# Depthwise weight gradient of a convolutional gate: products and sums on GpSimd in place of 128x128 products on TensorE, with new leads for the planner

## The chip, the cores and the metric

The kernel runs on one core of a Trainium2 chip. The metric is the device time of one execution in microseconds, as the median of several runs; a profile of one further execution shows where its time goes. PE is TensorE, PEld its weight loads, DVE VectorE, ACT ScalarE, POOL GpSimd, SP SyncE.

## The reference, cut to what matters

The reference is the forward pass and all gradients of an E-Branchformer block for B = 2 sequences of T = 4000 rows and D = 144 channels, in bf16. A global branch is attention; a local branch is a gated MLP whose gate is a depthwise convolution with K = 5 taps along the rows:

```python
xc = _layernorm(x, axis=-1)
h = _gelu(jnp.einsum('btd,de->bte', xc, w_mlp_in))
u, g = (h[..., :D].copy(), h[..., D:].copy())
g = _layernorm(g, axis=-1)
gp = jnp.pad(g, ((0, 0), (pad, pad), (0, 0)))
gc = jnp.zeros_like(g)
for i in range(K):
    gc = gc + gp[:, i:i + T, :] * dw_csgu[i][None, None, :]
loc = jnp.einsum('btd,de->bte', u * gc, w_mlp_out)
...
_out, _vjp = jax.vjp(_f, x, w_qkv, w_att_out, w_mlp_in, dw_csgu, w_mlp_out, dw_merge, w_merge)
_grads = _vjp(grad_out)
```

The change concerns the gradient of `dw_csgu`, a 5x144 result: for tap i and channel c it is the sum over all 8000 rows of gp[row + i, c] times dgc[row, c], where dgc is the gradient that reaches gc.

## The kernel before, in words

Rows are laid out in 32 blocks of 125 partitions per sequence (PB = 125, NB = 32), partition p of block j holding row 32 p + j, so that a shift by one row is a shift by one block, and halos are needed only at the ends. The kernel has a head (weights, layer norm, transposes), then one long loop over the 64 query blocks of both sequences (`phase_att`), and an end in which the merge convolution, the output, dx and the remaining weight gradients are computed.

In step s of the loop, TensorE makes the scores of block s and the dP tiles of block s-1 (`quad`: four products of 500 columns on L1254, then four of 16 rows on L1261, into the PSUM tiles `ps`, of which there are two). VectorE takes each score tile out with its negated minimum (`S_min`, L1276, into Pbuf); ScalarE takes the exponential (L1282); the dP tile is multiplied by P, either by VectorE straight from PSUM (L1290) or by ScalarE's copy (L1292) and a VectorE product in SBUF (L1294). Pbuf and Sbuf go through DMA transposes into PT and ST, from which `Y_half` (L1303) and `Z_half` (L1341) sum over 32 blocks. `X_group` (L1385) sums the gradient of the normalised input, which VectorE adds to `acc` (L1391). GpSimd makes small operands on the way: qr (L1237), QBs (L1321 to L1325).

Beside it, in the steps that are set aside for it, run the "local units" (`local_units`), 16 rounds of two blocks per batch, one batch after the other. In a round, blocks of a new pair n get their gelu and its derivative (L576 to L637, with the tiles l_hs, l_sq, l_a, l_z, l_th, l_q, l_hg), the normalised gate and dgc, which go side by side into a ring of tiles `gd` (gd[:, 0] the gate, gd[:, 1] dgc; five slots and three fixed ones for the ends), and the last 16 channels also into `gd_rem`. `t_unit` transposes them, `gc_unit` and `dgn_unit` make the convolution and its adjoint for an older pair o, `dhT_unit` transposes the gradient of h (dhr), and `dwi_unit` makes the gradient of w_mlp_in.

The weight gradient of the gate is made in `dwc_unit`, in every second round, over four blocks. For each block and tap it makes the 128x128 product of the shifted gate with dgc on TensorE; of this product only the diagonal is wanted. Part 0 holds four taps in one PSUM tile `pw` of 128x512 (L728), part 1 the fifth tap (L730) and one 80x144 product for the last 16 channels of all five taps (L731). `flush` copies the tile to `l_fl` with ScalarE (L710) and adds it to the accumulator `A_dwc` (128x784, f32) with GpSimd (L711). At the end `Final.dwc` takes the diagonals out: VectorE multiplies by the identity (L1873) or a mask (L1874) with a running sum, casts to bf16, two transposes on TensorE turn the columns into rows, and six transfers write the 5x144 result. `dwi_unit` uses `flush` as well, with 96x432 tiles.

The order of the work on each engine isn't the order of the program. `Planner.plan` takes the instructions from step 2 on, groups PE's, gives each group a duration from a table of costs (`cost`, and the lines at L1025 for groups), and lays them out one after another by a list schedule: of the groups that are ready it takes the one with the least key, and the key is its place in the program plus a lead from the table LEAD, by engine, output tile and size ("A" keys before the end stage, "T" keys in it). The chosen order is then fixed on every engine.

Of the kernel before, what the change touches and what calls it, by code (L numbers as in the profile page):

```python
# [8 lines left out]
BF = mybir.dt.bfloat16  # L9
F32 = mybir.dt.float32  # L10
ACT = mybir.ActivationFunctionType
ALU = mybir.AluOpType
# [3 lines left out]
D = 144  # L16
DR = 16
PB = 125
# [510 lines left out]
G2 = 2  # L529
# [4 lines left out]
def local_units(k, W, b, S, A, es, DHT, ps_w, gw):  # L534

    nc, tc = k.nc, k.tc
# [3 lines left out]
    pl = es.enter_context(tc.tile_pool(name="loc%d" % b, bufs=1, side=side, reuse_waits="tile"))  # L540
# [3 lines left out]
    rem = pl.tile([PB, 2, NB + 4, DR], BF, name="gd_rem")  # L544

    def gd(c):
        return gdr[{0: NR, NG2: NR + 1, NG2 + 1: NR + 2}.get(c, c % NR)]
    for c in (0, NG2 + 1):
        lo = 0 if c == 0 else 96
        nc.gpsimd.memset(gd(c)[lo:(32 if c == 0 else PB)], 0.0)  # L550
    gT = [pl.tile([128, 4, PB], BF, name="gT%d" % i) for i in range(4)]
# [11 lines left out]
    gc = pl.tile([PB, G2, D], BF, name="l_gc")  # L563
    dd = pl.tile([PB, G2, 2 * D], BF, name="l_dd")
    w_ = pl.tile([PB, G2, D], F32, name="l_w")
    fl = pl.tile([128, 512], F32, name="l_fl")

    def slot(g):
        return 3 if g == NG2 - 1 else g % 3
# [138 lines left out]
    def flush(ps, rows, acc):  # L708
        n = ps.shape[1]
        nc.scalar.copy(fl[0:rows, 0:n], ps)  # L710
        nc.gpsimd.tensor_tensor(acc, fl[0:rows, 0:n], acc, op=ALU.add)  # L711

    def blocks(g):
        return [(g - 1, 0), (g - 1, 1), (g, 0), (g, 1)]

    def gnb(h):
        return gd(h // G2)[:, 0, h % G2, 0:128]

    def dwc_unit(g, part):
        pw = ps_w.tile([128, 512], F32, tag="w")  # L720
        bl = blocks(g)
        for n_, (gg, bi) in enumerate(bl):
            i = G2 * gg + bi
            first, last = n_ == 0, n_ == len(bl) - 1
            t = gd(gg + 1)
            if part == 0:
                for kk in range(4):
                    nc.tensor.matmul(pw[:, kk * 128:(kk + 1) * 128], gnb(i + kk), t[:, 1, bi, 0:128], start=(first and kk == 0), stop=last, skip_group_check=True)  # L728
            else:
                nc.tensor.matmul(pw[:, 0:128], gnb(i + 4), t[:, 1, bi, 0:128], start=first, stop=last, skip_group_check=True)  # L730
                nc.tensor.matmul(pw[0:80, 128:128 + D], rem[:, 0, i:i + 5, :].rearrange("p a b -> p (a b)"), t[:, 1, bi, :], start=False, stop=last, skip_group_check=True)  # L731
        if part == 0:
            flush(pw[:], 128, A.dwc[:, 0:512])
        else:
            flush(pw[:, 0:128], 128, A.dwc[:, 512:640])
            flush(pw[0:80, 128:128 + D], 80, A.dwc[0:80, 640:784])

    def dwi_unit(g):
        pw = ps_w.tile([96, 3 * D], F32, tag="w")
# [12 lines left out]
    def round_(n, o, c):  # L752

        new = [(z_unit, n, 0), (z_unit, n, 1), (e_tanh, n), (e_h, n), (e_stats, n), (dug_unit, n), (e_gn, n), (e_dgc, n), (e_m, n), (e_gp, n)]
        old = [(gc_unit, o), (e_du, o), (dgn_unit, o), (e_dh, o)]
        end = [(dhT_unit, o)]
        if o is not None and o % 2:
            end += [(dwc_unit, o, 0), (dwc_unit, o, 1), (dwi_unit, o)]
        tr = [(t_unit, c, c - 2 if c is not None and c >= 2 else None)]
        if n is None:  # L760
            new = [None] * 10
        if o is None:
            old, end = [None] * 4, [None]
        if c is None:
            tr = [None]
        for u_ in (new[0:3] + old[0:1] + new[3:5] + old[1:2] + new[5:7] + old[2:3] + new[7:9] + old[3:4] + new[9:10] + tr + end):
            if u_ is not None:
                add(*u_)
# [11 lines left out]
class Planner:  # L780


    LEAD = {
# [13 lines left out]
    }  # L797


# [114 lines left out]
    def plan(self, i0, i1, window=400, late=1 << 40):  # L914
# [38 lines left out]
        for ins in todo:  # L953
            if ins.name not in gof:
                continue
            g = gof[ins.name]
# [66 lines left out]
        for g in groups:  # L1023
            d, end = 0.0, 0.0
            if g["e"] == "PE" and g["sg"]:  # L1025
                m = [i for i in g["ins"] if i.ins[0].bass_ap.ap[0][1] >= 128]
                if len(m) < len(g["ins"]):
                    d = len(m) * 0.21 + 0.094 + 0.22 + 0.14
                    end = d - 0.14 + 0.22
                else:  # L1030
                    d = len(m) * 0.21
                    end = d + 0.17
            else:
                for i in g["ins"]:
                    b, l = self.cost(g["e"], i)
                    end = d + l
                    d += b
            g["d"], g["end"] = d, end
        succ = [[] for _ in groups]
        need = [len(p) for p in preds]  # L1040
# [755 lines left out]
class Final:  # L1796
# [68 lines left out]
    def dwc(self):  # L1865

        k, nc, A, fp, W = self.k, self.k.nc, self.A, self.fp, self.W
        dwc_c = fp.tile([128, 5], F32, name="dwc_c")
        dwc_s = fp.tile([80, 1], F32, name="dwc_s")
        self.jf = jf = fp.tile([128, D], F32, name="jf")  # L1870
        av = A.dwc
        for kk in range(5):
            nc.vector.scalar_tensor_tensor(jf[:, 0:128], av[:, kk * 128:(kk + 1) * 128], 1.0, W.ident[:], op0=ALU.mult, op1=ALU.mult, accum_out=dwc_c[:, kk:kk + 1])  # L1873
        nc.vector.scalar_tensor_tensor(jf[0:80, 0:DR], av[0:80, 640 + 128:640 + D], 1.0, W.mask[:], op0=ALU.mult, op1=ALU.mult, accum_out=dwc_s[:])  # L1874
        dwc_b = fp.tile([128, 5], BF, name="dwc_b")
        nc.vector.tensor_copy(dwc_b[:], dwc_c[:])
        dwc_sb = fp.tile([80, 1], BF, name="dwc_sb")
        nc.vector.tensor_copy(dwc_sb[:], dwc_s[:])
        pt = self.pt([5, 128], BF)
        nc.tensor.transpose(pt[:], dwc_b[:], W.ident[:])  # L1880
        o5 = fp.tile([5, 128], BF, name="o5")
        nc.scalar.copy(o5[:], pt[:])
        nc.sync.dma_start(k.out5[:, 0:128], o5[:])
        pt = self.pt([1, 80], BF)
        nc.tensor.transpose(pt[:], dwc_sb[:], W.ident[0:80, 0:80])
        o5s = fp.tile([1, 5, DR], BF, name="o5s")
        nc.scalar.copy(o5s[:].rearrange("p a b -> p (a b)"), pt[:])
        for kk in range(5):
            nc.sync.dma_start(k.out5[kk:kk + 1, 128:D], o5s[:, kk, :])

    def qk(self):
        k, nc, A, fp, W = self.k, self.k.nc, self.A, self.fp, self.W
# [88 lines left out]
def kernel(ctx, tc, x, w_qkv, w_att_out, w_mlp_in, dw_csgu, w_mlp_out, dw_merge, w_merge, grad_out,  # L1981
# [47 lines left out]
    A = K()  # L2029
    A.dM1T = ap.tile([128, 2, D], F32, name="A_dM1T")  # L2030
    A.dWiT = ap.tile([96, 3 * D], F32, name="A_dWiT")
    A.dwc = ap.tile([128, 784], F32, name="A_dwc")
    k.ps_w = pool(ctx, "ps_w", "left", bufs=3, space=PSUM)
    k.ps_yz = pool(ctx, "ps_yz", "left", bufs=1, space=PSUM)
    W = K()
# [114 lines left out]
    F = Final(k, W, A, ar, fp)  # L2150
    F.ps = K()
    F.ps.tile = lambda shape, dt, tag=None, name=None, bufs=None: k.ps_w.tile(shape, dt, tag="w", name=name)
    side += [F.dwc, F.dwi, F.weights]
    for q, f in enumerate(M.tr_pieces(1)):
        f()
# [66 lines left out]
```

## Time and profile before

| | us |
|---|---|
| median of three runs | 1304.31 |
| lowest and highest | 1299.45, 1305.04 |
| the profiled execution | 1301.2 |
| its span in the profile | 1299.4 |
| PE idle in the span | 40.3 |
| products into pw from gd (L728, L730, L731), instructions | 384 |
| copies to l_fl for them (L710) | 18.2 |
| sums into A_dwc (L711) | 38.3 |

An instruction's row gives the smallest, the median and the largest duration, or the mean; a product on PE has a span of about 0.22 us, but products overlap, and the distance from one start to the next is what each takes of PE's time. Busy time on PE counts the union of such spans. A line "A <- B: us, times, longest" says how long engine A stood idle before an instruction and whose result ended that idle time.

### The profile page before, as it was taken

The page shows a single profiled execution, that of the slowest core. Times are in us where ns is not written, and L with a number is a line of the kernel's source. Part 1 is how long each engine was busy: PE and PEld are TensorE (multiplying, and loading weights), DVE is VectorE, ACT ScalarE, POOL GpSimd, SP SyncE. Part 2 cuts the span into 40 slices and gives each one's busy share as a digit, 9 for nine tenths or more (in the row PEclk, how much of TensorE's full clock was granted, in tenths as well). Part 3 has the DMA queues.
Part 4 walks back from the last instruction along what each step waited for, and adds up shares of the span by engine and source line. Part 5 has one row for each costly group of instructions (what it writes and reads, how often), then busy time and mean ns, then how long its engine had stood idle before and what let it go on. Part 6 is the DMA issues. An engine that isn't in the chain of part 4 may idle for free.

```text
span 1299.4 us, 39889 instructions
## 1 busy us (share of the span) xinstructions
PE 1259.1 (97%) x16190; PEld 1045.8 (80%) x16190; DVE 1053.7 (81%) x2808; ACT 828.5 (64%) x1384; POOL 505.6 (39%) x1013
## 2 busy tenths in 40 slices
PE   5999999999999999999999999999999999999998
PEld 3677888888888887877778888888888878799997
DVE  7589888888889888888978898888888887767925
ACT  4776676676676776556756767667566666436561
POOL 8654434443444433331444434344443423143310
PEclk8999999999999999999999999999999999999999
DMA  4587787687677687979987688777676868958702
GB/s 121 103 143 128 129 142 134 117 151 125 126 135 132 121 140 148 162 137 162 180 145 130 124 144 122 130 127 139 123 136 123 137 120 153 185 121 219 204 25 58
DMA packets 585444, 175.45 MB, mean 135 GB/s; under 512 B 560813, under 2 KB 579663, under 8 KB 585239
## 3 DMA queue, kind: packets, MB, share of 16 engines
q1 hardware_dynamic: 583544, 171.31, 71.6%
q8 instruction: 126, 2.06, 0.6%
q0 software_dynamic: 1168, 1.39, 0.4%
q14 instruction: 58, 0.48, 0.1%
q10 hardware_dynamic: 548, 0.21, 0.1%
HBM read 22.96 MB, written 16.69 MB: 31 GB/s over the span
## 4 chain that ended last, share of the span: by engine, by line
PE 87%; DVE 4%; DMA 2%; ACT 2%; POOL 2%; issue 2%; SPq 1%; ACTq 0%; DVEq 0%; POOLq 0%
PE X L1385 21%; PE ps L1254 15%; PE yz L1341 10%; PE yz L1303 9%; PE ps L1261 6%; PE Hps L1673 3%; PE po L1758 2%; PE pd L611 1%; PE pc L663 1%; PE pj L1227 1%; PE pd L678 1%; PE pt L1243 1%; ACT Pbuf L1282 1%; PE pw L728 1%; DVE Pbuf L1276 1%
## 5 line engine op out<-in xcount | busy, mean ns | idle before, releaser
L1276 DVE TENSOR_SCALAR_CACHE_REDUCE Pbuf<-ps 125x1000 bf16<-125x1000 f32 x256 | 306.4, 1197 | 92.3 <-PE ps L1261 87.5
L1282 ACT ACTIVATE Pbuf<-Pbuf,nm 125x1000 bf16<-125x1000 bf16 x256 | 282.6, 1134 | 79.0 <-DVE nm L1278 79.0
L1385 PE MATMUL X<-QBs,Sbuf 125*125 125x144 bf16 x2048 | 296.3, 228 | 0.3 <-ACT l_sq L579 0.2
L1385 PE MATMUL X<-QBs,Pbuf 125*125 125x144 bf16 x2048 | 291.4, 226 | 1.5 <-POOL QBs L1325 1.5
L1385 PEld LDWEIGHTS <-Sbuf 125*125 125x125 bf16 x2048 | 259.4, 137 | 20.8 <-issue 20.8
L1254 PE MATMUL ps<-xaT_m,qt 128*125 128x500 bf16 x1024 | 261.8, 375 | 2.5 <-ACT Sbuf L1292 1.2
L1385 PEld LDWEIGHTS <-Pbuf 125*125 125x125 bf16 x2048 | 260.5, 137 | 0.6 <-issue 0.5
L1292 ACT CAST Sbuf<-ps 125x1000 bf16<-125x1000 f32 x190 | 189.6, 998 | 100.1 <-PE ps L1261 99.8
L1391 DVE TENSOR_TENSOR acc<-X,acc 125x432 f32<-125x432 f32 (+1 forms) x373 | 201.4, 550 | 31.5 <-PE X L1385 27.8
L1254 PEld LDWEIGHTS <-qt 128*125 128x125 bf16 x1024 | 121.5, 136 | 43.3 <-issue 4.7
L1341 PE MATMUL yz<-xa_aug,ST 125*125 125x144 bf16 x2048 | 150.9, 228 | 3.9 <-ACT ty L1319 3.0
L1303 PE MATMUL yz<-xa_aug,PT 125*125 125x145 bf16 x2048 | 147.7, 227 | 4.2 <-DMA PT<-Pbuf 4.2
L1341 PEld LDWEIGHTS <-ST 125*125 125x125 bf16 x2048 | 139.9, 138 | 6.5 <-issue 5.5
L1303 PEld LDWEIGHTS <-PT 125*125 125x125 bf16 x2048 | 137.3, 137 | 8.3 <-DMA PT<-Pbuf 5.4
L1294 DVE TENSOR_TENSOR Sbuf<-Sbuf,Pbuf 125x1024 bf16<-125x1024 bf16 x190 | 134.6, 711 | 9.5 <-ACT Sbuf L1292 9.4
L1261 PEld LDWEIGHTS <-qt 16*125 16x125 bf16 x1024 | 36.6, 128 | 99.1 <-issue 98.4
L1261 PE MATMUL ps<-XR,qt 16*125 16x500 bf16 x1016 | 112.1, 420 | 0.0
L1321 POOL TENSOR_SCALAR QBs<-qb,rl 125x144 bf16<-125x144 bf16 x64 | 26.1, 408 | 181.4 <-DVE rl L1309 160.7
L1290 DVE TENSOR_TENSOR Sbuf<-ps,Pbuf 125x1000 bf16<-125x1000 f32 x66 | 78.8, 1194 | 6.5 <-PE ps L1261 3.4
L711 POOL TENSOR_TENSOR A_dwc<-l_fl,A_dwc 128x512 f32<-128x512 f32 (+2 forms) x48 | 38.3, 798 | 90.2 <-ACT l_fl L710 89.8
L1237 POOL COPY qr<-qb 125x64 bf16<-125x64 bf16 x124 | 31.9, 284 | 77.8 <-ACT qb L1229 75.3
L581 POOL TENSOR_SCALAR l_a<-l_sq 125x576 bf16<-125x576 bf16 x32 | 21.5, 672 | 95.4 <-ACT l_sq L579 94.7
(579 smaller groups left out, 2508.8 us busy)
## 6 DMA issues: line engine op xcount, KB each, us to landing
Yn_d<-yn SPq DMA_DIRECT2D x64, 35.2 KB
Zn_d<-zn SPq DMA_DIRECT2D x64, 35.2 KB
ug_d<-ugr SPq DMA_DIRECT2D x32, 70.3 KB
PT<-Pbuf SPq DMA_TRANSPOSE x126
ST<-Sbuf SPq DMA_TRANSPOSE x126
go_h<-in_grad_out_dram SPq DMA_DIRECT2D x8, 252.0 KB
Yg<-Yn_d SPq DMA_DIRECT2D x8, 252.0 KB
Yg<-ug_d SPq DMA_DIRECT2D x8, 252.0 KB
```

The costliest lines, as they stand in the source:

```text
L1254: mm = nc.tensor.matmul(pp[r // 2][:, r % 2, 0:CH], QT[i][:, 3 * h, :], bs(i)[0].xaT_m[:, c * CH:(c + 1) * CH], start=True, stop=False)
L1261: nc.tensor.matmul(pp[r // 2][:, r % 2, 0:CH], QT[i][rs, 1 + (q // 2 + h) % 2, :], xr, start=False, stop=True)
L1276: nc.vector.tensor_scalar(pv(Pbuf, i % NPB, c2), src, -1.0, 3.0e38, op0=ALU.mult, op1=ALU.min, accum_out=NM[i][:, c2:c2 + 1])
L1282: nc.scalar.activation(v, v, ACT.Exp, bias=NM[i][:, 4:5], scale=-1.0)
L1290: nc.vector.tensor_tensor(pv(Sbuf, i % NDB, c2), src, pv(Pbuf, i % NPB, c2), op=ALU.mult)
L1292: nc.scalar.copy(pv(Sbuf, i % NDB, c2), src)
L1294: nc.vector.tensor_tensor(sc, sc, pchunk(i % NPB, c2), op=ALU.mult)
L1303: nc.tensor.matmul(Y, PT[0:PB, j, 0:PB], S.xa_aug[:, j, 0:D + 1], start=(j == 0), stop=(j == NB - 1))
L1341: nc.tensor.matmul(Z, ST[0:PB, j, 0:PB], S.xa_aug[:, j, 0:D], start=(j == 0), stop=(j == NB - 1))
L1385: nc.tensor.matmul(X[:, jj, :], l, r, start=(n_ == 0), stop=(n_ == len(ops) - 1))
L1391: nc.vector.tensor_tensor(av, X[:, 0:nj, :], av, op=ALU.add)
L1673: nc.tensor.matmul(H[0:rows, a // 3, (a % 3) * D:(a % 3 + 1) * D], lhs, self.src[b][h][:, 2 + j, :], start=(n == 0 and a % 3 == 0), stop=( ...
```

## The change

`dwc_unit` no longer uses TensorE. It is called for each single block (twice in every round, where before two parts were called in every second round). GpSimd multiplies the gate, shifted by each of the five taps, with dgc, element by element over all 144 channels, into a new tile `l_pr` (125x5x144, f32): the taps of one gate tile go together, so that a block takes three products, two over 2x144 columns and one over 144. A fourth instruction adds l_pr to `A_dwc`, which now is 125x5x144 in f32. The sum over the 125 partitions is left to the end: `Final.dwc` splits A_dwc into a high and a low bf16 part on VectorE, in pieces of three and two taps, and TensorE multiplies both with a column of ones (the column D of xa_aug, `F.one`), giving one row of 432 or 288; ScalarE copies it out, and two transfers write the result.

`l_fl` shrinks to what `dwi_unit` needs. The table LEAD is replaced as a whole; in the planner's costs a group of quads with remainders gets 0.02 us more, and each PE group 0.02 us more.

```diff
-    fl = pl.tile([128, 512], F32, name="l_fl")
+    fl = pl.tile([96, 3 * D], F32, name="l_fl")
+    pr = pl.tile([PB, 5, D], F32, name="l_pr")
...
-    def dwc_unit(g, part):
-        pw = ps_w.tile([128, 512], F32, tag="w")
-        bl = blocks(g)
-        for n_, (gg, bi) in enumerate(bl):
-            i = G2 * gg + bi
-            first, last = n_ == 0, n_ == len(bl) - 1
-            t = gd(gg + 1)
-            if part == 0:
-                for kk in range(4):
-                    nc.tensor.matmul(pw[:, kk * 128:(kk + 1) * 128], gnb(i + kk), t[:, 1, bi, 0:128], start=(first and kk == 0), stop=last, skip_group_check=True)
-            else:
-                nc.tensor.matmul(pw[:, 0:128], gnb(i + 4), t[:, 1, bi, 0:128], start=first, stop=last, skip_group_check=True)
-                nc.tensor.matmul(pw[0:80, 128:128 + D], rem[:, 0, i:i + 5, :].rearrange("p a b -> p (a b)"), t[:, 1, bi, :], start=False, stop=last, skip_group_check=True)
-        if part == 0:
-            flush(pw[:], 128, A.dwc[:, 0:512])
-        else:
-            flush(pw[:, 0:128], 128, A.dwc[:, 512:640])
-            flush(pw[0:80, 128:128 + D], 80, A.dwc[0:80, 640:784])
+    def dwc_unit(g, bi):
+        i, t = G2 * g + bi, gd(g + 1)
+        kk = 0
+        while kk < 5:
+            h = i + kk
+            n = min(2 - h % 2, 5 - kk)
+            nc.gpsimd.tensor_tensor(pr[:, kk:kk + n, :], gd(h // G2)[:, 0, h % G2:h % G2 + n, :], t[:, 1, bi:bi + 1, :].to_broadcast([PB, n, D]), op=ALU.mult)
+            kk += n
+        nc.gpsimd.tensor_tensor(A.dwc[:], pr[:], A.dwc[:], op=ALU.add)
...
-        if o is not None and o % 2:
-            end += [(dwc_unit, o, 0), (dwc_unit, o, 1), (dwi_unit, o)]
+        if o is not None:
+            end += [(dwc_unit, o, 0), (dwc_unit, o, 1)]
+            if o % 2:
+                end += [(dwi_unit, o)]
...
     LEAD = {
-        "A PE ps 0 0": -120, "A DVE Pbuf 1000 0": 25, "A DVE Sbuf 1024 0": 175, "A PE ph 0": 40, "A ACT l_hs 288": 106, "A ACT l_sq 288": -167,
...
+        "A PE ps 0 0": -77, "A DVE Pbuf 1000 0": 135, "A ACT Sbuf 1000 0": 42, "A DVE Sbuf 1024 0": 178, "A PE ph 0": -199, "A ACT l_hs 288": -38,
...
-                    d = len(m) * 0.21 + 0.094 + 0.22 + 0.14
+                    d = len(m) * 0.21 + 0.094 + 0.22 + 0.16
                     end = d - 0.14 + 0.22
...
+                if g["e"] == "PE":
+                    d, end = d + 0.02, end + 0.02
...
-        for kk in range(5):
-            nc.vector.scalar_tensor_tensor(jf[:, 0:128], av[:, kk * 128:(kk + 1) * 128], 1.0, W.ident[:], op0=ALU.mult, op1=ALU.mult, accum_out=dwc_c[:, kk:kk + 1])
-        nc.vector.scalar_tensor_tensor(jf[0:80, 0:DR], av[0:80, 640 + 128:640 + D], 1.0, W.mask[:], op0=ALU.mult, op1=ALU.mult, accum_out=dwc_s[:])
...
-        for kk in range(5):
-            nc.sync.dma_start(k.out5[kk:kk + 1, 128:D], o5s[:, kk, :])
+        self.jf = fp.tile([128, D], F32, name="jf")
+        for a0, a1 in ((0, 3), (3, 5)):
+            n = (a1 - a0) * D
+            av = A.dwc[:, a0:a1, :].rearrange("p a b -> p (a b)")
+            hi, lo = (fp.tile([PB, 3 * D], BF, tag="dwc_%s" % t, name="dwc_%s" % t) for t in ("hi", "lo"))
+            nc.vector.tensor_copy(hi[:, 0:n], av)
+            nc.vector.tensor_tensor(lo[:, 0:n], av, hi[:, 0:n], op=ALU.subtract)
+            pt = self.pt([1, 3 * D], F32)
+            for q, t in enumerate((hi, lo)):
+                nc.tensor.matmul(pt[:, 0:n], self.one, t[:, 0:n], start=(q == 0), stop=(q == 1))
+            o5 = fp.tile([1, 3, D], BF, tag="o5", name="o5")
+            nc.scalar.copy(o5[:, 0:a1 - a0, :].rearrange("p a b -> p (a b)"), pt[:, 0:n])
+            nc.sync.dma_start(k.out5[a0:a1].rearrange("(o a) b -> o a b", o=1), o5[:, 0:a1 - a0, :])
...
-    A.dwc = ap.tile([128, 784], F32, name="A_dwc")
+    A.dwc = ap.tile([PB, 5, D], F32, name="A_dwc")
...
+    F.one = SS[1].xa_aug[:, 0, D:D + 1]
```

More of the change, by code (lines that the diff above doesn't have):

```diff
@@ L714, in blocks @@
         return [(g - 1, 0), (g - 1, 1), (g, 0), (g, 1)]
-    def gnb(h):
-        return gd(h // G2)[:, 0, h % G2, 0:128]
-    def dwc_unit(g, part):
-        pw = ps_w.tile([128, 512], F32, tag="w")
-        bl = blocks(g)
-        for n_, (gg, bi) in enumerate(bl):
-            i = G2 * gg + bi
-            first, last = n_ == 0, n_ == len(bl) - 1
-            t = gd(gg + 1)
-            if part == 0:
-                for kk in range(4):
-                    nc.tensor.matmul(pw[:, kk * 128:(kk + 1) * 128], gnb(i + kk), t[:, 1, bi, 0:128], start=(first and kk == 0), stop=last, skip_group_check=True)
-            else:
-                nc.tensor.matmul(pw[:, 0:128], gnb(i + 4), t[:, 1, bi, 0:128], start=first, stop=last, skip_group_check=True)
-                nc.tensor.matmul(pw[0:80, 128:128 + D], rem[:, 0, i:i + 5, :].rearrange("p a b -> p (a b)"), t[:, 1, bi, :], start=False, stop=last, skip_group_check=True)
-        if part == 0:
-            flush(pw[:], 128, A.dwc[:, 0:512])
-        else:
-            flush(pw[:, 0:128], 128, A.dwc[:, 512:640])
-            flush(pw[0:80, 128:128 + D], 80, A.dwc[0:80, 640:784])
+    def dwc_unit(g, bi):
[7 more added lines that the diff above has]
+        nc.gpsimd.tensor_tensor(A.dwc[:], pr[:], A.dwc[:], op=ALU.add)
     def dwi_unit(g):
@@ L1867, in dwc @@
         k, nc, A, fp, W = self.k, self.k.nc, self.A, self.fp, self.W
[L1868 to L1871, printed above, removed]
-        for kk in range(5):
-            nc.vector.scalar_tensor_tensor(jf[:, 0:128], av[:, kk * 128:(kk + 1) * 128], 1.0, W.ident[:], op0=ALU.mult, op1=ALU.mult, accum_out=dwc_c[:, kk:kk + 1])
-        nc.vector.scalar_tensor_tensor(jf[0:80, 0:DR], av[0:80, 640 + 128:640 + D], 1.0, W.mask[:], op0=ALU.mult, op1=ALU.mult, accum_out=dwc_s[:])
[L1875 to L1887, printed above, removed]
-        for kk in range(5):
-            nc.sync.dma_start(k.out5[kk:kk + 1, 128:D], o5s[:, kk, :])
+        self.jf = fp.tile([128, D], F32, name="jf")
[11 more added lines that the diff above has]
+            nc.sync.dma_start(k.out5[a0:a1].rearrange("(o a) b -> o a b", o=1), o5[:, 0:a1 - a0, :])
     def qk(self):
```

23 rows, old and new, of the table LEAD are left out of this document.

## The prediction, before the changed kernel had run

> **What bounds the kernel now.** I read the page first (busy times, chain), then busy time over the two windows in which the gate's work runs (66 to 507 us and 635 to 1092 us: the "local rounds", batch 0 and batch 1, beside attention), then the tile pw, in which the removed products are summed, then PE's timeline around one such unit, then the waits and the tiles where GpSimd and VectorE meet.
>
> ```profile
> PE 1259.1 (97%) x16190; PEld 1045.8 (80%) x16190; DVE 1053.7 (81%) x2808; ACT 828.5 (64%) x1384; POOL 505.6 (39%) x1013
> PE 87%; DVE 4%; DMA 2%; ACT 2%; POOL 2%; issue 2%; SPq 1%; ACTq 0%; DVEq 0%; POOLq 0%
> ```
> PE is busy almost all the time and holds 87% of the chain that ended last. In the two windows it is closer still:
>
> ```profile
> 66.00:507.00 441.00, 437.02 (x5579) 359.70 (x5578) 377.27 (x968) 299.62 (x492) 185.45 (x363) 1.00 0.75 132
> 635.00:1092.00 457.00, 452.74 (x5792) 373.20 (x5790) 386.96 (x987) 306.23 (x501) 183.80 (x359) 1.00 0.76 132
> ```
> The columns are the length, then PE, PEld, DVE, ACT and POOL busy. Over the 898 us of both, PE is idle 8.2 us, DVE is busy 764 (85%), ACT 606, POOL 369 (41%); the granted clock is 1.00. PE waits for nobody here, and others wait for it:
>
> ```profile
> DVE Pbuf L1276 <- PE ps L1261: 87.5, 133, 2.5
> ```
> VectorE stood idle 87.5 us in all for score tiles. So a PE instruction taken out of these windows shortens them, unless another engine comes up to PE.
>
> **What is removed.** Each of 16 units (8 per batch) issues 16 products on L728, and 4 each on L730 and L731: 384 in all.
>
> ```profile
> 154.93 0.28 PE L728 MATMUL pw<-gd,gd 125*128 125x128 bf16 x2
> ...
> 155.82 0.22 PE L730 MATMUL pw<-gd,gd 125*128 125x128 bf16 x1
> ...
> 156.29 0.38 PE L1254 MATMUL ps<-xaT_m,qt 128*125 128x500 bf16 x1
> ```
> A single product has a span of 0.22 us, but they overlap; the price is the distance between starts. The 16 of L728 take 155.82 - 154.93 = 0.89 us, the eight others 156.29 - 155.82 = 0.47 us: 1.36 us a unit, 21.8 us for 16. All of it lies on PE's path: -21.8. ScalarE loses 48 copies to l_fl (9.5 + 4.3 + 4.4 = 18.2 us by shape) and GpSimd 48 sums (20.4 + 8.9 + 9.0 = 38.3 us). ScalarE isn't near its limit, so I count nothing for the copies; the work that hides them is PE's, and if PE were not the bound they would be worth up to 18 us.
>
> **What is added on GpSimd.** For each of 64 blocks of 125 rows: two products of 125x288, one of 125x144 (bf16 in, f32 out), then one sum of 125x720 in f32. The order of the changed kernel shows both blocks of a round spread over GpSimd's queue between the old instructions. No row has these shapes; the two-input rows give the price:
>
> ```profile
> L1325 POOL TENSOR_TENSOR QBs<-g,g x64: 479/488/1038, 60.8 to 1152.5; 125x144 bf16<-125x144 f32 x64
> L711 POOL TENSOR_TENSOR A_dWiT<-l_fl,A_dWiT x16: 1091/1098/1243, 160.3 to 1091.7; 96x432 f32<-96x432 f32 x16
> ```
> Medians of 0.488 us at 144 columns and 1.098 at 432 are 2.1 ns a column over 0.18 us. So 288 columns cost 0.79, 144 0.48 and 720 1.70 us: 2 x 0.79 + 0.48 + 1.70 = 3.76 us a block, 241 us for 64. The least it could be: products at the price of the one-input copy of 288 columns (L601, median 0.424) and half of that for 144, 1.06 + 1.70 = 2.76 us, 177 us. I take 241, since the products have two inputs. All of the old sums (156.7 to 1089.8 us) and of the new work fall in the windows, so POOL there goes from 369 to about 369 - 38 + 241 = 572 of 876 us (65%): still far from full.
>
> **What this does to VectorE.** The two engines hold each other up:
>
> ```profile
> 436.33 1.10 POOL L711 TENSOR_TENSOR A_dWiT<-l_fl,A_dWiT 96x432 f32<-96x432 f32 x1 [2.00 <-ACT l_fl L710]
> 436.45 1.53 DVE L1294 TENSOR_TENSOR Sbuf<-Sbuf,Pbuf 125x1024 bf16<-125x1024 bf16 x1
> ```
> L1294 took 1.53 us where its median is 0.684: it started inside a GpSimd sum and ended 0.55 us after that sum. Others with two SBUF inputs show it too:
>
> ```profile
> L1294 DVE TENSOR_TENSOR Sbuf<-Sbuf,Pbuf x190: 651/684/1530, 52.3 to 1140.5; 125x1024 bf16<-125x1024 bf16 x190
> L590 DVE TENSOR_TENSOR l_hg<-l_q,l_hs x32: 444/460/919, 68.9 to 1026.9; 125x576 bf16<-125x576 bf16 x32
> L666 DVE TENSOR_TENSOR ugr<-ur,l_gc x32: 291/307/769, 113.1 to 1075.7; 125x288 bf16<-125x288 bf16 x32
> L1276 DVE TENSOR_SCALAR_CACHE_REDUCE Pbuf<-ps x256: 1161/1201/1204, 22.4 to 1129.8; 125x1000 bf16<-125x1000 f32 x128
> ```
> L1276, which reads PSUM, never grows (1.204 at most). Mean (from the groups by shape) less median, times count, over the ten two-input lines (L1294 0.027 x 190 = 5.1, L590 3.7, L666 2.9, seven others 3) is about 15 us now.
>
> How much more? Per us the windows hold about 0.5 such instructions (nine lines of 32 and some 150 of L1294 in 898 us). If all arrived at random and waited for the rest of the GpSimd instruction they met, then before: 369 us x 0.5 = 185 hits x 0.32 us (half of 0.65 us, the mean of POOL's durations in the windows, each weighted by itself) = 59 us. The trace has 15, one quarter, because GpSimd's work is often what VectorE had waited for anyway. For the added work: 241 us x 0.5 = 120 hits x 0.58 us (sums of 1.70 weigh most: weighted mean 1.16) = 70 us. Lower bound 0, upper bound 70; I take a quarter, 18 us. VectorE then has 764 + 18 = 782 us of 876 (89%; 95% at the upper bound).
>
> The Trainium skill bears on this (page "SBUF — State Buffer", section "SBUF: two separate sides"): the port pair of VectorE and GpSimd is a lock held for a whole instruction, the loser blocks fully, and a VectorE instruction with two SBUF inputs is among those that need it. L1294's 1.53 us agrees. Taken to the letter it speaks against this change and for the upper bound: by it the time would be the second rival's, by the quarter the sum's below.
>
> Does PE feel it? What is late next is the L1276 queued behind a blocked L1294: it empties ps, of which there are two. VectorE's idle time before L1276 (87.5 us in the run) is the cover. I let a quarter of the 18 us come through: +4.5; bounds 0 and 18.
>
> **Order, planner, end.** New leads and 0.02 us more per PE group in the planner's costs change the order on every engine; no wait is added apart from GpSimd's for its own products before each sum. Queued behind it stand qr (which PE's transposes wait for), l_q (L590 waits for it) and gd. The bounds of a new order: the windows' 8.2 us of PE idle time gone, or doubled: -8 to +8; I take 0, as no row favours a sign. At the end the diagonals' 5 masked sums and two transposes give way to two casts, two subtractions and four one-row products of 432 or 288 columns (about 0.18 and 0.12 us from L1254's 0.21 us for 500): 0.6 - 0.1 = +0.5 us on PE; four small transfers fewer, hidden by the output's.
>
> **Sum.** 1301.2 (the profiled execution; its span is 1299.4) - 21.8 + 4.5 + 0.5 = 1284.4. The median of the runs is 1304.3, 3.1 above the profiled one: 1287.5, forecast 1287 (-1.3%). Own range: 1287 - 8 to 1287 + 8 for the order, 1279 to 1296 with the stalls.
>
> **Rivals.**
> - *The stalls shrink as well* (0.15): ScalarE has 18 us less and the PSUM ring "w" 32 tiles fewer, so PE's waits in the windows vanish and the new order gains some in the stretches at 500 to 660 us and 1100 to 1140 us, where PE idles 7.8 + 3.7 us. 1287 - 4.5 - 8 = 1275. Against: nothing in these stretches is touched but order.
> - *VectorE becomes the bound through the lock* (0.14): 764 + 70 = 834 us of work in the windows. Its idle time was 134 us; if 75 of them stay (the waits for ACT, for first tiles and for PE's bursts), the windows last 909, 11 more than now: 1304 + 11 = 1315. It decides from about 764 + 37 us of VectorE work on, where VectorE's 801 plus 75 pass PE's 876. For it: long GpSimd sums, and the single wait of 0.98 us above; against: the quarter seen now.
> - *GpSimd's queue is late* (0.13): it is in order, and a qr, l_q or gd behind a block's 3.76 us comes late for PE. If each of the 32 rounds loses 0.6 us on PE, 19 us return and the time is 1287 + 19 - 4 = 1302, no change. The same time comes out if the products filled gaps that PE has anyway. Against both: 8.2 us of idle PE in 898, and GpSimd free a third of the time.
>
> **How the numbers follow.** Forecast 0.58, the rivals 0.15, 0.14, 0.13. What a measurement can tell is about 0.5%, 6.5 us: under 1297.8 is faster. Faster: 0.58 + 0.15 = 0.73; same 0.13; slower 0.14. The range takes in the first rival's 1275 with 4 us below it, and the third, and half of the way to the second: 1271 to 1308.
>
> **What would show it.** No pw group of L728's kind on PE; PE's instructions 382 fewer; PE's idle time in the two windows still about 8 us and the windows together near 880 us; l_pr at 0.79 and 0.48 us and A_dwc's 720 columns at 1.70; POOL near 705 us in the run; the two-input VectorE lines 15 to 20 us above their medians' sum more than now; VectorE's wait for ps still the longest of its waits. I am wrong if PE waits for DVE or POOL by more than 15 us in the windows, if L1294's mean passes 0.9 us, or if PE's busy time doesn't fall.

## The result and the profile after

The changed kernel takes 1320.1 us in the median (1319.6 to 1321.4) against 1304.7 us before, measured beside it: a ratio of 1.0126, 95% interval 1.0103 to 1.0149. It is 1.3% slower, clear of the noise; 1287 us had been forecast. The profiled execution took 1321.4 us, its span 1319.7. Lines of the attention loop stand eight lower than before (L1294 is L1286, L1276 is L1268), those of the gate's work one higher (L590 is L591).

First the page: busy time per engine, and the chain that ended last, by engine.

```profile
PE 1256.5 (95%) x15808; PEld 1032.2 (78%) x15808; DVE 1107.7 (84%) x2798; ACT 812.5 (62%) x1336; POOL 716.7 (54%) x1221
PE 56%; DVE 22%; DMA 6%; ACT 5%; issue 5%; POOL 4%; SPq 1%; DVEq 0%; ACTq 0%; POOLq 0%
```

TensorE has its 382 instructions less, but its busy time fell by only 2.6 us (from 1259.1); GpSimd has its work more (505.6 to 716.7 us). And VectorE, which has ten instructions fewer, is busy 54 us longer, and its share of the chain went from 4% to 22%. Then the two windows of the gate's work (length, then PE, PEld, DVE, ACT, POOL busy):

```profile
66.00:507.00 441.00, 422.17 (x5276) 343.61 (x5275) 400.63 (x958) 286.61 (x461) 290.95 (x459) 1.00 0.74 130
640.00:1095.00 455.00, 443.26 (x5543) 360.77 (x5543) 412.85 (x985) 296.38 (x473) 287.72 (x462) 1.00 0.76 133
```

In 896 us PE now idles 31 us where it idled 8, and 21 of them are waits for VectorE or GpSimd (before: 5). VectorE is busy 813 us, 91%, where it was busy 85%. GpSimd's 579 us are close to what had been worked out (572). The granted clock is 1.00 in both windows, as before. In the list of waits (idle us, times, longest), VectorE's wait for score tiles shrank from 87.5 to 63.1 us, and a wait the other way is now the largest of PE's. First its line of the kernel before, then both lines after:

```profile
PE ps L1254 <- DVE Pbuf L1276: 0.4, 1, 0.4
```

```profile
DVE Pbuf L1268 <- PE ps L1253: 63.1, 83, 5.0
PE ps L1246 <- DVE Pbuf L1268: 10.2, 19, 1.0
```

The new work itself, by the tile l_pr (smallest, median, largest duration in ns), costs close to what the rows of before had said (0.79 us for 288 columns, 1.70 for 720):

```profile
L723 POOL TENSOR_TENSOR l_pr<-gd x64: 721/728/1253, 119.0 to 1083.3; 125x288 f32<-125x288 bf16 x64
L725 POOL TENSOR_TENSOR A_dwc<-l_pr,A_dwc x64: 1697/1712/2182, 121.4 to 1085.7; 125x720 f32<-125x720 f32 x64
```

What grew are VectorE's instructions with two SBUF inputs. By tile:

```profile
L1286 DVE TENSOR_TENSOR Sbuf<-Sbuf,Pbuf x190: 652/686/2206, 55.1 to 1150.6; 125x1024 bf16<-125x1024 bf16 x190
L591 DVE TENSOR_TENSOR l_hg<-l_q,l_hs x32: 433/668/1961, 72.5 to 1040.3; 125x576 bf16<-125x576 bf16 x32
```

The smallest durations are those of before within 0.01 us, and the largest have grown: 2.21 us for 1.53, 1.96 for 0.92. The median of l_hg went from 0.46 to 0.67 us, that of Sbuf stayed (0.69). One such place in the timeline of the two engines:

```profile
337.88 2.03 POOL L725 TENSOR_TENSOR A_dwc<-l_pr,A_dwc 125x720 f32<-125x720 f32 x1
338.25 2.20 DVE L1286 TENSOR_TENSOR Sbuf<-Sbuf,Pbuf 125x1024 bf16<-125x1024 bf16 x1
339.88 1.10 POOL L590 TENSOR_SCALAR l_q<-l_th 125x576 bf16<-125x576 bf16 x1
```

VectorE's product started 0.37 us into the sum and ended at 340.45, 0.54 us after the sum's end at 339.91. The sum itself took 2.03 and not 1.71 us: a VectorE product with two SBUF inputs (l_z, 0.45 us) had begun at the same moment, 337.88. And l_q behind it, beside the rest of VectorE's product, took 1.10 us where its median is 0.67. Each engine waits for the other.

### The profile page after: what moved, and what is told of

The parts are those of the page before. It is cut to its first block, busy times and chain, and to the rows that moved or that the text cites. A ratio compares the mean times of both kernels' runs of the same rounds, so it can differ in the third digit from the quotient of the medians.

```text
span 1319.7 us, 39328 instructions
## 1 busy us (share of the span) xinstructions
PE 1256.5 (95%) x15808; PEld 1032.2 (78%) x15808; DVE 1107.7 (84%) x2798; ACT 812.5 (62%) x1336; POOL 716.7 (54%) x1221
## 4 chain that ended last, share of the span: by engine, by line
PE 56%; DVE 22%; DMA 6%; ACT 5%; issue 5%; POOL 4%; SPq 1%; DVEq 0%; ACTq 0%; POOLq 0%
PE X L1377 13%; PE ps L1246 10%; PE yz L1333 7%; PE yz L1295 6%; DVE Pbuf L1268 5%; PE ps L1253 5%; DVE acc L1383 3%; DVE Sbuf L1286 3%; DMA ST<-Sbuf 2%; ACT Pbuf L1274 2%; PE po L1750 2%; PE Hps L1665 2%; DVE Sbuf L1282 1%; DVE l_hg L591 1%; DMA out_dram<-dxo 1%
## 5 line engine op out<-in xcount | busy, mean ns | idle before, releaser
L1268 DVE TENSOR_SCALAR_CACHE_REDUCE Pbuf<-ps 125x1000 bf16<-125x1000 f32 x256 | 305.6, 1194 | 64.5 <-PE ps L1253 63.1
L1246 PE MATMUL ps<-xaT_m,qt 128*125 128x500 bf16 x1024 | 264.6, 378 | 11.4 <-DVE Pbuf L1268 10.2
L1286 DVE TENSOR_TENSOR Sbuf<-Sbuf,Pbuf 125x1024 bf16<-125x1024 bf16 x190 | 152.0, 800 | 16.1 <-ACT Sbuf L1284 15.6
L725 POOL TENSOR_TENSOR A_dwc<-l_pr,A_dwc 125x720 f32<-125x720 f32 x64 | 114.4, 1788 | 2.9
L1315 POOL TENSOR_SCALAR g<-qb,rl 125x144 f32<-125x144 bf16 x64 | 26.9, 420 | 140.5 <-DVE rl L1301 112.2
L723 POOL TENSOR_TENSOR l_pr<-gd,gd 125x288 f32<-125x288 bf16 (+1 forms) x128 | 83.3, 657 | 2.0
L1229 POOL COPY qr<-qb 125x64 bf16<-125x64 bf16 x124 | 34.8, 311 | 52.1 <-ACT qb L1221 51.4
```

Of the source, the lines that this page charges most:

```text
L725: nc.gpsimd.tensor_tensor(A.dwc[:], pr[:], A.dwc[:], op=ALU.add)
L1246: mm = nc.tensor.matmul(pp[r // 2][:, r % 2, 0:CH], QT[i][:, 3 * h, :], bs(i)[0].xaT_m[:, c * CH:(c + 1) * CH], start=True, stop=False)
L1268: nc.vector.tensor_scalar(pv(Pbuf, i % NPB, c2), src, -1.0, 3.0e38, op0=ALU.mult, op1=ALU.min, accum_out=NM[i][:, c2:c2 + 1])
L1286: nc.vector.tensor_tensor(sc, sc, pchunk(i % NPB, c2), op=ALU.mult)
```

## The experiments

Three theories had to be told apart: GpSimd's reads hold VectorE up (the lock); GpSimd's queue is longer, so that what stands behind the new work comes late; the new leads and costs make a worse order by themselves. In all runs called "order held", the planner accounts for the cut or added instructions as for those that they stand for, so that PE (but for left-out products), DVE, ACT and SP issue the same instructions in the same order as the kernel they are made from.

**The new work with the old leads and costs (e1).** Only LEAD and the two costs go back.

```diff
-        "A PE ps 0 0": -77, "A DVE Pbuf 1000 0": 135, "A ACT Sbuf 1000 0": 42, "A DVE Sbuf 1024 0": 178, "A PE ph 0": -199, "A ACT l_hs 288": -38,
...
+        "A PE ps 0 0": -120, "A DVE Pbuf 1000 0": 25, "A DVE Sbuf 1024 0": 175, "A PE ph 0": 40, "A ACT l_hs 288": 106, "A ACT l_sq 288": -167,
...
-                    d = len(m) * 0.21 + 0.094 + 0.22 + 0.16
+                    d = len(m) * 0.21 + 0.094 + 0.22 + 0.14
-                if g["e"] == "PE":
-                    d, end = d + 0.02, end + 0.02
```

> The new work (products and sums on GpSimd) with the old kernel's leads and planner costs. If the loss comes from GpSimd holding VectorE up, wherever the work stands in the queue: VectorE's busy time stays 45 to 65 us above the 1053.7 of before and the time is 1310 to 1325. If it comes from the new leads and costs: about 1304.7 - 21.8 + 5 = 1288. If GpSimd's lateness for others is the cause: like the changed kernel, 1315 to 1325, with VectorE's busy time near 1070.

Measured: 1343.9 us, ratio 1.032 (1.0274 to 1.0366); VectorE busy 1105.3 us. VectorE's busy time is as the lock has it, but the time is above all three expectations: with the old leads the new work loses 24 us more. So the new leads aren't the cause of the loss.

**The old work with the new leads and costs (e2).** The same exchange in the kernel before.

> The old work (products on TensorE) with the new leads and planner costs. If the new order costs nothing by itself: 1297 to 1312. If the new order is the loss: 1304.7 + 22 to 37, thus 1325 to 1340. The first 60 us, which no lead touches, tell whether their 4 us come from the run or the order: 4 us later here as well would speak for something other than GpSimd.

Measured: 1330.8 us, ratio 1.0206 (1.0169 to 1.0243); VectorE busy 1046.2. The new order costs the old work 27 us. That is the range of "the new order is the loss", but e1 excludes that reading: there the new work without the new order is slower still. So each set of leads fits the work that it came with, and a foreign set costs 24 to 27 us: far more than the 8 us that the prediction had allowed for order. PE's busy time rose to 1274.7 us with the instructions of before (1259.1), so an order can add busy time and not only idle time. As to the delay of 4 us in the first 60: the third block's first score tile left VectorE 2.9 us later than in the kernel before (in the changed kernel 3.9). That speaks neither for GpSimd nor for the order: the run e7 below has the order of before and was 4.1 us late at the same place.

**Short sums, order held (e3).** The changed kernel; products and sums run over one column.

```diff
-            nc.gpsimd.tensor_tensor(pr[:, kk:kk + n, :], gd(h // G2)[:, 0, h % G2:h % G2 + n, :], t[:, 1, bi:bi + 1, :].to_broadcast([PB, n, D]), op=ALU.mult)
+            p = nc.gpsimd.tensor_tensor(pr[:, kk:kk + n, 0:1], gd(h // G2)[:, 0, h % G2:h % G2 + n, 0:1], t[:, 1, bi:bi + 1, 0:1].to_broadcast([PB, n, 1]), op=ALU.mult)
-        nc.gpsimd.tensor_tensor(A.dwc[:], pr[:], A.dwc[:], op=ALU.add)
+        p = nc.gpsimd.tensor_tensor(A.dwc[:, :, 0:1], pr[:, :, 0:1], A.dwc[:, :, 0:1], op=ALU.add)
```

> The changed kernel with each product and sum on GpSimd cut to the first column of 144, its planned cost held, so that the order on the engines stays; the gate's weight gradient is left out but for that column. Both theories of GpSimd (holding VectorE up; late for others) expect most of the loss back: 1283 to 1293, VectorE's busy time back to 1055 to 1065. If the order is the cause: above 1305 still.

Measured: 1287.9 us, ratio 0.9873 (0.9842 to 0.9904). The page's busy times:

```profile
PE 1243.7 (97%) x15808; PEld 1026.6 (80%) x15808; DVE 1042.4 (81%) x2798; ACT 813.2 (63%) x1336; POOL 516.3 (40%) x1221
```

With GpSimd's time gone (716.7 to 516.3 us; 256 instructions of 0.2 us remain) VectorE is back at 1042.4 us, below the range that was expected. GpSimd's added time thus costs 32.2 us (1320.1 - 1287.9), and without it the new work in its own order is 16.1 us faster than the kernel before: no loss is left for the order to explain. What the new order gives or takes beside the removed products these runs don't separate. That the time is the forecast's 1287 is chance, since the forecast had counted 4.5 us for the lock, which is nearly gone here. PE's busy time is 12.8 us less than in the changed kernel, with the same instructions in the same order: part of the loss stood there as busy time of PE.

**The same time without the reads, order held (e4).** As e3; behind each short product or sum GpSimd writes zeros into l_pr, for about the time that was cut.

```diff
+                m = nc.gpsimd.memset(pr[:].rearrange("p a b -> p (a b)")[:, x0:x0 + n], 0.0)
...
+            fill(p, kk * D, *((288, 120) if n == 2 else (144,)))
...
+        fill(p, 0, 720, 720, 96)
```

> As the run with short sums, but GpSimd then writes zeros into the product tile for about the time that the product or sum had taken (its queue is as long as in the changed kernel, 690 to 730 us busy), without reading SBUF; the gradient is left out but for one column. If the reads of two inputs hold VectorE up: VectorE's busy time 1055 to 1070, its product of 1024 columns near 0.70 us in the mean, time 1283 to 1297. If GpSimd's queue is what is late: 1312 to 1322, as changed.

Measured: 1300.0 us (1298.6 to 1302.9), ratio 0.9982 (0.9965 to 1.0000). Page, then waits, then the tile Sbuf:

```profile
PE 1252.7 (96%) x15808; PEld 1031.0 (79%) x15808; DVE 1042.5 (80%) x2798; ACT 814.5 (63%) x1336; POOL 704.7 (54%) x1733
```

```profile
DVE rsr L617 <- POOL rsr L601: 11.8, 13, 1.4
DVE l_hg L591 <- POOL l_q L590: 9.5, 13, 1.8
DVE l_dd L695 <- POOL l_w L689: 8.9, 9, 2.7
```

```profile
L1310 DVE TENSOR_TENSOR Sbuf<-Sbuf,Pbuf x190: 651/685/1150, 53.4 to 1134.0; 125x1024 bf16<-125x1024 bf16 x190
```

GpSimd is as busy as in the changed kernel, within 12 us, but VectorE isn't: 1042.5 us, as with short sums, and no product of 1024 columns above 1.15 us. So the reads are what makes VectorE's instructions longer: 65 us of its time (1107.7 - 1042.5), 20.1 us of the kernel's (1320.1 - 1300.0). That the zeros come in pieces of at most 0.70 us isn't the reason: with the sum in pieces of 0.49 us that read, VectorE's time stays high (e5, below). The other 12.1 us (1300.0 - 1287.9) come from the length of GpSimd's queue, and the waits name them: VectorE stands 30 us before results of GpSimd (rsr, l_q, l_w), 3 us in e3. In the changed kernel these waits are 7.5 us only, since there VectorE itself is late; the 12.1 us are the price of the queue where the lock is away, and the two parts are told apart by taking them away one after the other. Both theories hold, each for its part; the expectation, which had the one or the other, wasn't met: the time lies between its two ranges, and VectorE's busy time below that of the reads.

**The sum in five pieces, order held (e5).**

```diff
-        nc.gpsimd.tensor_tensor(A.dwc[:], pr[:], A.dwc[:], op=ALU.add)
+        for kk in range(5):
+            m = nc.gpsimd.tensor_tensor(A.dwc[:, kk, :], pr[:, kk, :], A.dwc[:, kk, :], op=ALU.add)
```

> The changed kernel, its order held, with the sum of 720 columns made as five sums of 144, one after another. GpSimd is busy longer (five of about 0.48 us in place of one of 1.71: +45 us, some 760 us in all). If what VectorE waits for is the end of the one instruction that holds it: its busy time falls from 1107.7 to 1075 to 1090 and the time is 1305 to 1317. If VectorE has to wait until GpSimd has nothing to do: its busy time is not lower, and the time 1322 to 1340. If GpSimd's lateness for others were the main thing: 1325 and more.

Measured: 1334.9 us, ratio 1.0231 (1.0180 to 1.0282); POOL busy 765.1, DVE 1092.0 us. VectorE's busy time fell by 16 us, a little less than expected of a hold by single instructions, and the time rose by 15, into the ranges of the other two. The rise points to GpSimd's queue, which is 48 us longer: GpSimd's share of the chain went from 4% to 21%, and VectorE's waits for rsr, l_q and l_w from 7.5 to 29.6 us.

```profile
PE 51%; POOL 21%; DVE 13%; ACT 7%; DMA 4%; issue 4%; SPq 0%; ACTq 0%; DVEq 0%; POOLq 0%
```

In most places VectorE gets its turn after the GpSimd instruction that it met. Here its product got in among five sums that follow one another without a gap; the five took 2.73 us, where five that nothing holds up take 2.26:

```profile
116.67 2.73 POOL L726 TENSOR_TENSOR A_dwc<-l_pr,A_dwc 125x144 f32<-125x144 f32 x5
118.13 0.93 DVE L1306 TENSOR_TENSOR Sbuf<-Sbuf,Pbuf 125x1024 bf16<-125x1024 bf16 x1
```

But not always. The worst place:

```profile
481.25 0.73 POOL L723 TENSOR_TENSOR l_pr<-gd 125x288 f32<-125x288 bf16 x1
481.41 5.12 DVE L1306 TENSOR_TENSOR Sbuf<-Sbuf,Pbuf 125x1024 bf16<-125x1024 bf16 x1
481.93 2.26 POOL L726 TENSOR_TENSOR A_dwc<-l_pr,A_dwc 125x144 f32<-125x144 f32 x5
484.15 0.46 POOL L723 TENSOR_TENSOR l_pr<-gd,gd 125x144 f32<-125x144 bf16 x1
484.57 0.73 POOL L723 TENSOR_TENSOR l_pr<-gd 125x288 f32<-125x288 bf16 x1
485.25 0.73 POOL L723 TENSOR_TENSOR l_pr<-gd,gd 125x288 f32<-125x288 bf16 x1
```

VectorE's product stood through nine GpSimd instructions that followed each other without a gap, and ended at 486.53, 0.55 us after the last of them. Counted over the trace, 139 VectorE instructions with two SBUF inputs took over 0.15 us longer than the shortest of their kind: 128 waited only for the GpSimd instruction that was running, 6 for one or two whole ones more, 5 for three to eight more.

**Products whole, sums short, order held (e6).** Of e3's edit only the sum's.

> The changed kernel, its order held, products whole and only the sum cut to the first column (the gradient is left out but for that column). By the square of the durations the sums hold seven tenths of the lock's cost and by time just under half of GpSimd's: if the lock's cost goes with single long instructions, 1295 to 1302 and VectorE's busy time 1058 to 1068; if it goes with GpSimd's busy time, about the middle between 1288 and 1320, 1304, and 1075.

Measured: 1294.4 us, ratio 0.9920 (0.9897 to 0.9944); DVE busy 1059.7, POOL 612.7. That is 0.6 us below the range that was expected of a cost that goes with single long instructions, and far from the 1304 of one that goes with busy time: the sums, 46% of the time added on GpSimd (114.4 of 248 us), make 25.7 of the 32.2 us, and 48 of VectorE's 65.

**Fewer products on TensorE, order held (e7).** The kernel before, with one block in four.

```diff
-        bl = blocks(g)
+        bl = blocks(g)[3:]
```

> The kernel before, its order held, with one of the four blocks of each unit in the products on TensorE (96 of 384 instructions; the gradient's other three quarters are left out). It takes 16.3 us of TensorE's work away and nothing else. If TensorE is the bound there, as predicted: 1304 - 16 = 1288, 1285 to 1292. If its time was hidden beside VectorE or the waits: 1298 to 1304.

Measured: 1295.4 us (1290.1 to 1296.2) against 1305.1, ratio 0.9921 (0.9891 to 0.9951): 9.7 us for 16.3 us of PE's work, between the two ranges that were expected. TensorE bounds the windows, but not for every microsecond: about six tenths come through, by the interval of the ratio four to nine.

**A planner that knows the lock (e8).**

```diff
+                        if ok and lock[g] and cur[other[e]] and free_t[other[e]] > now + 1e-9:
+                            ok = False
```

> The changed kernel with a planner that doesn't start a VectorE instruction with two SBUF inputs while a GpSimd instruction that reads SBUF runs in its own account, nor the other way round; leads and costs as in the changed kernel. If the lock's cost comes from a plan that is blind to it: VectorE's busy time falls under 1085 and the time under 1315. If no order avoids it with this much work: 1315 to 1335. A new order alone has been worth 24 to 27 us here, so a time above 1320 with a low busy time of VectorE would be the order's.

Measured: 1355.9 us, ratio 1.0395 (1.0370 to 1.0421); VectorE busy 1083.3. This order does avoid part of the lock's cost (24 of 65 us of VectorE's time), and the time is 36 us longer all the same. The expectation puts such a time down to the order, under leads that were chosen for another one; the run doesn't show it apart. Whether leads chosen for this planner would make it worthwhile wasn't tried.

**The old leads once more: short sums (e10), and writes for the same time (e11).** The edits of e3 and e4 in e1.

> The new work with the old leads and costs (that run took 1343.9), its order held, products and sums cut to the first column as in the run with short sums (the gradient is left out but for that column). If GpSimd's added time costs the same in any order, some 32 us: 1308 to 1315, and the old leads lose their 20 to 25 us on this work without GpSimd's help. If the old leads are bad only because they place GpSimd's long work badly: 1285 to 1295.

> As the run before it, with GpSimd writing for the time that its products and sums had taken, reading almost nothing. If the reads hold VectorE up by the same amount in any order: about 20 us under 1343.9, 1318 to 1328, VectorE's busy time 1040 to 1050. If the old order loses through GpSimd's lateness and not through the lock: 1335 to 1345.

Measured: 1312.3 us (1303.4 to 1316.1), ratio 1.0067 (1.0039 to 1.0094), and 1323.4 us, ratio 1.0136 (1.0083 to 1.0189), VectorE busy 1049.8 and 1049.7. With the medians of the others:

| GpSimd's new work | new leads, us | old leads, us |
|---|---|---|
| short (e3, e10) | 1287.9 | 1312.3 |
| as long, writes (e4, e11) | 1300.0 | 1323.4 |
| as it is (changed kernel, e1) | 1320.1 | 1343.9 |

Both times are in the ranges expected of a cost that is the same in any order. The steps down the columns are 12.1 and 20.1 us, and 11.1 and 20.5 us, in two orders that differ by 24 us in every row. So close an agreement is partly chance, since the runs were taken at three times and single runs differ by several us. By each run's ratio to the kernel before, measured beside it, the steps are 14 and 19 us, and 9 and 24: both parts are there in both orders, and their sizes are known to some 5 us.

## Why the prediction was wrong, step by step

- *TensorE bounds the windows*: right in the main (e7), but the step took every microsecond: 1.36 us a unit, 21.8 in all, at face value. By e7's six tenths it is some 13 us; with the new order, and GpSimd's time out of the way, 16.1 came (1287.9 against 1303.9 beside it).
- *The cost on GpSimd*: right. 3.76 us a block were worked out from rows of other shapes, and the medians give 2 x 0.73 + 0.46 + 1.71 = 3.63; 572 us busy in the windows were forecast, 579 measured, in which GpSimd's own waiting for VectorE is included (the new instructions took 248 us, 232 by their medians).
- *What this does to VectorE*: the step that failed. The mechanism, GpSimd's reads holding up VectorE's instructions with two SBUF inputs, was seen in the row of 1.53 us, and the estimate for arrivals at random was 70 us. The prediction then took a quarter of it, 18 us, because before the change only a quarter was in the trace. Measured: 65 us for the added work, by e4 (against the kernel before, which had 38 us of old sums, VectorE's busy time rose by 54). The quarter didn't carry over. A likely reason, argued and not shown: the old GpSimd instructions mostly start when VectorE delivers their input and VectorE waits for what they return, so that the two rarely meet; the new ones depend on tiles that were ready long before, and fall anywhere. The Trainium skill's rule (page "SBUF — State Buffer", section "SBUF: two separate sides"), weighed and set aside for the quarter, was the better guide: a full block for the loser, and only against GpSimd instructions that read SBUF. Both are in the runs: 2.20 us for a product of 0.69, and VectorE's 1042.5 us busy when GpSimd only writes.
- *Does PE feel it*: 4.5 us were forecast, 20.1 came. Of 65 us that is three tenths, so the quarter that was let through was about right and the size of the work wasn't. No row had shown that quarter, which was a choice between bounds: its nearness is luck.
- *GpSimd's queue*: priced at nothing in the sum, because GpSimd would be free a third of the time: the second step that failed. It costs 12.1 us by e4, and not by the way that the third rival gave (results late for TensorE) but through VectorE, which waits for rsr, l_q and l_w. That L590 waits for l_q the prediction had seen, and given no price.
- *The order*: taken as 0, with 8 us either way. For the change as a whole nothing here speaks against 0, though no run prices it alone; but the bound of 8, from PE's idle time, was far too small: a foreign set of leads costs 24 to 27 us, and in e2 PE's busy time grew by 15.6 us with the same instructions, which no bound from idle time holds.
- *The rivals*: the second, VectorE held up by the lock, was forecast at 1315 us with a chance of 0.14, and is the larger part of what happened; the third, by way of VectorE and not of TensorE, is the smaller part. The prediction let them exclude each other, though one cause, more GpSimd time, feeds both.
- *The signs of being wrong*: the first came, PE's waits for VectorE or GpSimd in the windows, 21 us where 15 was the limit. The other two didn't: the mean of L1294 (now L1286) is 0.80 us, under 0.9, and PE's busy time fell, if only by 2.6 us.

The sum as it came: 1303.9 - 16.1 (TensorE's work, in the new order) + 12.1 (queue) + 20.1 (lock) = 1320.0. It must close, since each term is a difference of two runs that stand next to each other. Against the forecast's terms the lock is 15.6 us more, the queue 12.1 more, and the gain on TensorE, with the end, 5.2 less: 32.9 of the 33 us that were missed. Why a set of leads costs 24 to 27 us on the other's work is open; it was measured, not taken apart.

## What to carry to other kernels

Work moved to GpSimd beside a busy VectorE was paid for twice here, with GpSimd busy for two thirds of the windows only: VectorE's instructions with two SBUF inputs waited for GpSimd instructions that read SBUF, and GpSimd's longer queue delivered its small results late. The first can be estimated by arrivals at random: added busy time, times the rate of such VectorE instructions (0.5 per us here), times half of the added instructions' mean duration, in which each duration counts by its own length. With the medians as measured this estimate gives 67 us of VectorE's time for the changed kernel, 20 for e6 and 39 for e5; measured, against e3, were 65, 17 and 50. So don't scale it down by what other work on GpSimd shows. And before the order of a planned kernel is called neutral, price it by giving the old work the new order.

## What the runs showed of the hardware that had not been expected

VectorE can be passed over in a row of GpSimd instructions that follow one another without a gap: 5.12 us for a product of 0.69, through nine GpSimd instructions of 0.45 to 0.73 us (e5). Mostly it isn't: in the same run 128 of 139 lengthened instructions waited only for the GpSimd instruction that was running, and in the changed kernel VectorE's product of 2.20 us got in between the sum and l_q, which follows without a gap. The Trainium skill (page "SBUF — State Buffer", section "SBUF: two separate sides") speaks of a lock for the whole of one instruction, for whichever starts first; that fits the 128, and not the 5 that three to eight whole instructions passed, where the measurement decides. What settles who comes next is open. These five places make e5's cost larger than the estimate above, but cutting a long GpSimd instruction into short ones does lower VectorE's busy time, by 16 us here; the longer queue cost more than that.
